# Attention sums in four column tiles with reciprocals by way of DRAM, a new order in the step, and five PSUM banks for attention where there were four

## Chip, cores, metric

One core of one Trainium2 chip. The metric is device time of one execution, in microseconds (us). A kernel's time is the median of its runs.

## The reference

Eight batches of attention over 12 heads (448 positions, head size 64), q and k normalised, then a two-layer MLP on 3584 tokens with `h - tanh(h)` between the layers; all float32.

```python
batch, n_heads, seq, head_dim = (8, 12, 448, 64)
n_tokens, d_model, d_ff = (3584, 768, 2048)
q_n, k_n = rmsnorm(q, g_q), rmsnorm(k, g_k)
attn = exp(scale * q_n @ k_n.T - max)            # per batch and head
attn = attn / (sum(attn, axis=-1) + 1e-09)
x = (attn @ v).transpose(0, 2, 1, 3).reshape(B * S, H * D)
h = x @ w_in
out = (h - tanh(h)) @ w_out
```

## The kernel before

A step is two heads of one batch: six steps make a batch, 48 steps the kernel. The MLP multiplies each layer but the second one of batch 0 as seven half-size products in place of eight (numbered 1 to 7; they run in the order 1, 4 of the tile pair before, 5, 6, 2, 7, 3). `run(gap)` emits MLP products of the batch before for so many nanoseconds. So attention is woven into the MLP from step 6 on; steps 0 to 5 (`first_slot`) have no MLP to hide in.

The kernel has eight PSUM banks in use: four hold attention, and `ma`, `mc` and two `mb` the MLP:

```python
ps_s = pool("ps_s", bufs=4, space=PSUM)
ps_m = pool("ps_m", bufs=1, space=PSUM)

def mm_bank(tag):
    return ps_m.tile([P, 512], F32, name=tag, bufs=2 if tag == "mb" else 1)
```

The sums over keys: one matmul per head with ones as weights, 64 equal rows per head, so that the reciprocal stands ready for a plain product with the values:

```python
def totals(s, dn):
    ...                                # parts: one added-up tile, or four in the first steps
    for i, p in enumerate(parts):
        for h in range(2):
            nc.tensor.matmul(
                dn[h * D : (h + 1) * D, :S], lhsT=ones[:CP, :D], rhs=p[:, h, :],
                start=(i == 0), stop=(i == len(parts) - 1),
            )
    rd = sp.tile([P, S], F32, name="rd")
    nc.vector.reciprocal(rd, dn[:, :S])
    return rd

def slot(s):                           # one woven step
    gap = gap_ns(s)
    scores(s + 1, 0); load(s + 2, "v")
    run(gap)
    norm(s + 3)                        # VectorE and GpSimd; ends with GpSimd's pow
    rd = totals(s, sc_bank())
    divide(s, values(s, sc_bank()), rd)
    run(gap)
    scores(s + 1, 1); add(s + 1)
    run(gap)
    turn(s + 2, sc_bank(), sc_bank()); norm_q(s + 3); load(s + 4, "kq")
    run(gap)
```

To evict a product is to read its sums out of its bank, which frees the bank for the next one.

```python
def factors(first):                    # operands of products 4 to 6 of the second layer
    ...
    if first:
        nc.vector.tensor_tensor(out=f1, in0=g12, in1=g11, op=ALU.subtract)     # writes tg
        nc.vector.tensor_tensor(out=f2, in0=g22, in1=f1, op=ALU.subtract)      # writes tg
        nc.gpsimd.tensor_tensor(out=g12, in0=g22, in1=g12, op=ALU.subtract)
    ...
elif p == 6:
    nc.vector.tensor_tensor(out=s2, in0=v, in1=s1, op=ALU.add)                 # evicts bank mb; then 7 adds to it
...
elif p == 3:
    nc.vector.tensor_tensor(out=s2, in0=v, in1=s2, op=ALU.add)
    def rest():                        # emitted after the next product
        shrink(up, high, s2, nc.gpsimd)                                        # writes gT
        factors(True)
    late["todo"].append(rest)
elif p == 4:
    nc.vector.tensor_tensor(out=s1, in0=v, in1=s1, op=ALU.add)                 # evicts bank mb
```

## Time and profile before

1589.97 us, median of three runs (1589.63 to 1591.56). For the comparison I cut a profiled run in three: **start**, up to the MLP's first product of batch 0; **middle**, batch 0's MLP and batch 1's first layer, up to the first `ma<-gT` product, with which batch 1's second layer begins; **weave**, from there to the last such product, with the last 33 of the 42 woven steps and a tail of plain products. In this kernel they take 120.4, 344.8 and 1105.7 us; 17.7 follow.

The page's slices of the kernel before (40 slices of 39.7 us, TensorE's busy tenths and granted clock), then from the waits of TensorE between 440 and 1480 us the only row (engine, line, what it waited for: us in all, times, longest) and one of these waits in order of time (in brackets the idle time before the instruction, and what ended it), then the reciprocals' row of the page's groups:

```profile
PE   3988768998999999999999999999999999999997
PEclk9999879999999999999999999999999999999999
```
```profile
PE mb L448 <- DVE s L530: 8.1, 6, 1.4
```
```profile
637.05 1.78 PE L448 MATMUL mb<-xT,w_f 128*128 128x224 f32 x8 [1.35 <-DVE s L530]
```
```profile
L400 DVE RECIPROCAL rd<-sc 128x448 f32<-128x448 f32 x42 | 124.0, 2953 | 34.9 <-PE sc L395 34.0
```

TensorE is full from the eighth slice or so on. From 440 to 1480 us it waits 8 us, for one thing: VectorE's line 530, the eviction of product 6, before product 7 may add to the same bank.

### The profile page before, as it was taken

Reading aid. Unit: us, or ns where it says so; the run is one execution under the profiler, and the core shown is the slowest. Engines: PE = TensorE matmul, PEld = TensorE weight load, DVE = VectorE, ACT = ScalarE, POOL = GpSimd, SP = SyncE. Lnnn points to the kernel's source line nnn. Section 1 sums busy time; section 2 is a strip of 40 time slices with the busy share of each in tenths; the row PEclk is TensorE's granted clock in tenths of the full one; section 3 lists DMA queues with packets and bytes.
Section 4 is the critical chain, followed back from the end, with each engine's and each line's share of the span. In section 5 each row is a group of like instructions: output and inputs, shape, how many; then the busy total and the mean of one; then the engine's idle time right before and its main releaser. Section 6 shows DMA issues by size and latency. Waiting matters only on the chain.

```text
span 1588.6 us, 19983 instructions
## 1 busy us (share of the span) xinstructions
PE 1494.3 (94%) x7440; PEld 1164.7 (73%) x7440; DVE 788.6 (50%) x1004; ACT 446.4 (28%) x870; POOL 624.4 (39%) x516
## 2 busy tenths in 40 slices
PE   3988768998999999999999999999999999999997
PEld 1336456446878878878877887787877887789997
DVE  6788558865454345434544445434544344522211
ACT  4554234512322223222331232321331232210210
POOL 6655446552452234422453235423444234311410
PEclk9999879999999999999999999999999999999999
DMA  7554575577545554555554564465454664455564
GB/s 193 177 181 165 195 256 166 138 196 229 164 141 161 147 151 144 152 166 148 154 170 123 158 177 131 147 184 139 137 167 133 171 166 137 135 152 162 174 196 105
DMA packets 253983, 257.80 MB, mean 162 GB/s; under 512 B 143413, under 2 KB 198709, under 8 KB 253877
## 3 DMA queue, kind: packets, MB, share of 16 engines
q1 hardware_dynamic: 253552, 256.43, 55.4%
q8 instruction: 61, 1.00, 0.3%
q14 instruction: 46, 0.37, 0.1%
q10 hardware_dynamic: 324, 0.00, 0.0%
HBM read 223.35 MB, written 33.03 MB: 161 GB/s over the span
## 4 chain that ended last, share of the span: by engine, by line
PE 74%; DVE 13%; POOL 3%; DMA 3%; issue 2%; ACT 2%; SPq 2%; ACTq 0%; DVEq 0%; POOLq 0%
PE mb L448 24%; PE ma L448 16%; PE mc L448 15%; PE sc L357 8%; PE sc L383 6%; DVE rd L400 2%; DVE w_out L79 2%; PE sc L395 2%; POOL sq L310 2%; DVE sum L376 2%; DMA w_f<-w_in 1%; PE mb L616 1%; DVE rr L311 1%; ACT p L362 1%; DVE w_out L82 1%
## 5 line engine op out<-in xcount | busy, mean ns | idle before, releaser
L362 ACT ACTIVATE p<-sc,rr 112x448 f32<-112x448 f32 x384 | 212.5, 638 | 224.0 <-PE sc L357 162.0
L448 PE MATMUL mb<-tt,w_f 128*128 128x224 f32 x768 | 166.5, 361 | 17.3 <-DMA w_f<-w_in 16.3
L357 PE MATMUL sc<-qT,kT 64*112 64x448 f32 x768 | 179.5, 574 | 2.2 <-DVE rd L400 1.5
L448 PE MATMUL ma<-xT,w_f 128*128 128x224 f32 x768 | 163.8, 365 | 11.9 <-DMA w_f<-w_in 11.9
L448 PEld LDWEIGHTS mb<-tt,w_f 128*128 128x128 f32 x768 | 142.6, 192 | 42.6 <-issue 22.8
L448 PEld LDWEIGHTS ma<-xT,w_f 128*128 128x128 f32 x768 | 149.7, 197 | 18.7 <-issue 6.2
L315 POOL TENSOR_TENSOR rr<-rr,neg_half 112x16 f32<-112x16 f32 (+1 forms) x49 | 140.7, 2871 | 51.3 <-DVE rr L314 50.3
L400 DVE RECIPROCAL rd<-sc 128x448 f32<-128x448 f32 x42 | 124.0, 2953 | 34.9 <-PE sc L395 34.0
L448 PE MATMUL ma<-gT,w_f 128*128 128x224 f32 x672 | 139.2, 356 | 0.0
L448 PEld LDWEIGHTS ma<-gT,w_f 128*128 128x128 f32 x672 | 125.3, 190 | 15.3 <-issue 15.3
L448 PE MATMUL mb<-tg,w_f 128*128 128x224 f32 x672 | 135.1, 354 | 0.0
L383 PE MATMUL sc<-p,v_nat 112*64 112x448 f32 x672 | 133.4, 539 | 0.0
L448 PEld LDWEIGHTS mb<-tg,w_f 128*128 128x128 f32 x672 | 126.2, 190 | 7.3 <-issue 7.3
L376 DVE TENSOR_TENSOR sum<-sum,p 112x896 f32<-112x896 f32 x80 | 95.8, 1198 | 58.2 <-ACT p L362 52.6
L357 PEld LDWEIGHTS sc<-qT,kT 64*112 64x112 f32 x768 | 65.9, 176 | 79.4 <-issue 62.1
L535 POOL TENSOR_TENSOR u<-u,s 128x448 f32<-128x448 f32 x32 | 36.5, 1141 | 221.0 <-DVE u L534 194.7
L311 DVE TENSOR_REDUCE rr<-sq 112x8 f32<-112x512 f32 x96 | 65.4, 681 | 113.9 <-POOL sq L310 113.9
L310 POOL TENSOR_TENSOR sq<-q_nat 112x512 f32<-112x512 f32 x48 | 50.0, 1041 | 150.5 <-DVE rr L311 103.2
L383 PEld LDWEIGHTS sc<-p,v_nat 112*64 112x64 f32 x672 | 48.3, 137 | 78.0 <-issue 78.0
L448 PE MATMUL mb<-xT,w_f 128*128 128x224 f32 x384 | 87.4, 366 | 17.2 <-DVE s L530 11.4
L504 POOL TENSOR_TENSOR gT<-s,th 128x448 f32<-128x448 f32 x64 | 75.0, 1172 | 62.1 <-ACT th L503 62.1
L448 PEld LDWEIGHTS mb<-xT,w_f 128*128 128x128 f32 x384 | 71.3, 194 | 34.6 <-issue 20.4
(108 smaller groups left out, 2146.0 us busy)
## 6 DMA issues: line engine op xcount, KB each, us to landing
w_f<-w_in SPq DMA_DIRECT2D x224, 384.0 KB, 3.6
w_f<-w_out SPq DMA_DIRECT2D x147, 512.0 KB, 4.3
w_raw<-in_moe_w_out_dram SPq DMA_DIRECT2D x32, 384.0 KB, 3.4
k_nat<-in_k_dram SPq DMA_DIRECT2D x96, 112.0 KB, 3.3
q_nat<-in_q_dram SPq DMA_DIRECT2D x48, 224.0 KB, 3.7
v_nat<-in_v_dram SPq DMA_DIRECT2D x48, 224.0 KB, 4.7
w_in<-w_out SPq DMA_DIRECT2D x28, 384.0 KB, 5.6
out_dram<-th SPq DMA_DIRECT2D x192, 56.0 KB, 2.7
```

Of the source, the lines that this page charges most:

```text
L79: nc.vector.tensor_scalar(out=bits, in0=bits, scalar1=4, scalar2=1, op0=ALU.logical_shift_left, op1=ALU.logical_shift_right)
L310: nc.gpsimd.tensor_tensor(out=sq, in0=rows, in1=rows, op=ALU.mult)
L311: nc.vector.reduce_sum(rr[:, "kq".index(name)], sq, axis=AX.X)
L315: nc.gpsimd.tensor_tensor(out=r, in0=r, in1=neg_half[:, : r.shape[1]], op=ALU.pow)
L357: nc.tensor.matmul(sc[:CP, :S], lhsT=kT[r, c * CP : (c + 1) * CP], rhs=qT[r, :], start=True, stop=True)
L362: nc.scalar.activation(p[:, h, i, :], tiles[h][:CP, :S], AF.Exp, scale=rr[:, 0, 2 * c + h : 2 * c + h + 1])
L376: nc.vector.tensor_tensor(out=t, in0=t, in1=part, op=ALU.add)
L383: nc.tensor.matmul(av[h * D : (h + 1) * D, :S], lhsT=v_nat[:, h, c, :], rhs=p[:, h, c % 2, :], start=(c == 0), stop=(c == NCH - 1),)
L400: nc.vector.reciprocal(rd, dn[:, :S])
L448: nc.tensor.matmul(bank[:, f * HS : (f + 1) * HS], lhsT=w[:, f * depth + c, :], rhs=moving[p](c), start=(first and f == 0 and c == 0), sto ...
L504: eng.tensor_tensor(out=g[:, rows, cols], in0=h, in1=th, op=ALU.subtract)
L535: nc.gpsimd.tensor_tensor(out=u3, in0=u3, in1=s5, op=ALU.add)
```

## The change

Its intent: sums in four column tiles of 32 columns (head and half of the queries) need half of TensorE's time and leave a reciprocal of half the width. The price is that each reciprocal stands on 32 rows where 64 are wanted, for half of the queries; a small store to DRAM and a load that repeats each row put that right. Sums and values each move beside half of the scores, so that there are fewer switches of tiling. And attention gets a fifth PSUM bank, taken from `mb`.

```diff
-    ps_s = pool("ps_s", bufs=4, space=PSUM)
+    ps_s = pool("ps_s", bufs=5, space=PSUM)
-        return ps_m.tile([P, 512], F32, name=tag, bufs=2 if tag == "mb" else 1)
+        return ps_m.tile([P, 512], F32, name=tag)
 ...                                                       # totals
-                nc.tensor.matmul(
-                    dn[h * D : (h + 1) * D, :S], lhsT=ones[:CP, :D], rhs=p[:, h, :], ...
+                for n in range(2):
+                    r = (2 * h + n) * BL
+                    nc.tensor.matmul(
+                        dn[r : r + BL, :HS], lhsT=ones[:CP, :BL], rhs=p[:, h, n * HS : (n + 1) * HS], ...
-        rd = sp.tile([P, S], F32, name="rd")
-        nc.vector.reciprocal(rd, dn[:, :S])
+        rs = whole[s] = sp.tile([P, HS], F32, name="rs")
+        nc.vector.reciprocal(rs, dn[:, :HS])
+    def rows_out(s):
+        row = whole[s] = scratch.tile([2, S], F32, name="row", bufs=2)
+        nc.sync.dma_start(out=row..., in_=rs.rearrange("(g i) q -> g i q", i=BL)[:, 0, :])
+    def rows_in(s):
+        rd = whole[s] = sp.tile([P, S], F32, name="rd")
+        nc.sync.dma_start(
+            out=rd,
+            in_=bass.AP(tensor=row.tensor, offset=row.offset, ap=[[S, 2], [0, D], [1, S]]),
+        )
 ...                                                       # first_slot
+        totals(s, mm_bank("mc"))                           # now first of all
         scores(s + 1, 0)
-        turn(s + 2, mm_bank("mb"), mm_bank("mb"))
+        turn(s + 2, mm_bank("mb"), sc_bank())
         load(s + 4, "kq"); norm(s + 3); weight(ahead - 2)
-        rd = totals(s, mm_bank("mc"))
         load(s + 2, "v")
+        rows_out(s)
         weight(ahead - 1)
+        rows_in(s)
         scores(s + 1, 1); add(s + 1)
 ...                                                       # slot
+        totals(s, sc_bank())
         scores(s + 1, 0); load(s + 2, "v")
-        run(gap)
+        run(gap / 2)
+        rows_out(s)
         norm(s + 3)
-        rd = totals(s, sc_bank())
-        divide(s, values(s, sc_bank()), rd)
+        run(gap / 2)
+        rows_in(s)
+        turn(s + 2, sc_bank(), sc_bank()); load(s + 4, "kq")
         run(gap)
+        divide(s, values(s, sc_bank()))
         scores(s + 1, 1); add(s + 1)
         run(gap)
-        turn(s + 2, sc_bank(), sc_bank()); load(s + 4, "kq")
         norm_q(s + 3)
         run(gap)
```

More of the change, by code (lines that the diff above doesn't have):

```diff
@@ L298, in ring_load @@
                 nc.sync.dma_start(out=t, in_=w_out_dram[:, BLOCKS[p], j].rearrange("p f d -> p (f d)"))
-    normed, turned, probs, sums, xT, tt = {}, {}, {}, {}, {}, {}
+    normed, turned, probs, sums, whole, xT, tt = {}, {}, {}, {}, {}, {}, {}
     def norm(s):
@@ L394, in totals, with divide @@
             for h in range(2):
-                nc.tensor.matmul(
-                    dn[h * D : (h + 1) * D, :S], lhsT=ones[:CP, :D], rhs=p[:, h, :],
-                    start=(i == 0), stop=(i == len(parts) - 1),
-                )
-        rd = sp.tile([P, S], F32, name="rd")
-        nc.vector.reciprocal(rd, dn[:, :S])
-        return rd
-    def divide(s, av, rd):
+                for n in range(2):
+                    r = (2 * h + n) * BL
+                    nc.tensor.matmul(
+                        dn[r : r + BL, :HS], lhsT=ones[:CP, :BL], rhs=p[:, h, n * HS : (n + 1) * HS],
+                        start=(i == 0), stop=(i == len(parts) - 1),
+                    )
+        rs = whole[s] = sp.tile([P, HS], F32, name="rs")
+        nc.vector.reciprocal(rs, dn[:, :HS])
+    def rows_out(s):
+        rs = whole[s]
+        row = whole[s] = scratch.tile([2, S], F32, name="row", bufs=2)
+        nc.sync.dma_start(
+            out=row.rearrange("h (n q) -> (h n) q", n=2), in_=rs.rearrange("(g i) q -> g i q", i=BL)[:, 0, :]
+        )
+    def rows_in(s):
+        row = whole[s]
+        rd = whole[s] = sp.tile([P, S], F32, name="rd")
+        nc.sync.dma_start(
+            out=rd,
+            in_=bass.AP(tensor=row.tensor, offset=row.offset, ap=[[S, 2], [0, D], [1, S]]),
+        )
+    def divide(s, av):
         b, hp = steps[s]
+        rd = whole.pop(s)
         x = xT[b, hp] = xp.tile([P, S], F32, name="xT")
@@ L663, in first_slot @@
     def first_slot(s):
+        if has(s):
+            totals(s, mm_bank("mc"))
         if has(s + 1):
@@ L673, in first_slot @@
         weight(ahead - 2)
-        if has(s):
-            rd = totals(s, mm_bank("mc"))
         if has(s + 2):
             load(s + 2, "v")
+        if has(s):
+            rows_out(s)
         weight(ahead - 1)
+        if has(s):
+            rows_in(s)
         if has(s + 1):
@@ L682, in first_slot @@
         if has(s):
-            divide(s, values(s, mm_bank("ma" if s < NP - 1 else "mb")), rd)
+            divide(s, values(s, mm_bank("ma" if s < NP - 1 else "mb")))
         if has(s + 3):
@@ L693, in slot @@
             load(s + 2, "v")
-        run(gap)
+        run(gap / 2)
+        rows_out(s)
         if has(s + 3):
             norm(s + 3)
-        rd = totals(s, sc_bank())
-        divide(s, values(s, sc_bank()), rd)
+        run(gap / 2)
+        rows_in(s)
+        if has(s + 2):
+            turn(s + 2, sc_bank(), sc_bank())
+        if has(s + 4):
+            load(s + 4, "kq")
         run(gap)
+        divide(s, values(s, sc_bank()))
         if has(s + 1):
@@ L703, in slot @@
         run(gap)
-        if has(s + 2):
-            turn(s + 2, sc_bank(), sc_bank())
         if has(s + 3):
             norm_q(s + 3)
-        if has(s + 4):
-            load(s + 4, "kq")
         run(gap)
```

## The prediction

> **What bounds the kernel now.** I read the page first, then busy time in stretches, the chain of waits, TensorE's weight loads in order of time, and VectorE and the DMA issues of the first 120 us.
>
> ```profile
> PE 1494.3 (94%) x7440; PEld 1164.7 (73%) x7440; DVE 788.6 (50%) x1004; ACT 446.4 (28%) x870; POOL 624.4 (39%) x516
> ...
> PE 74%; DVE 13%; POOL 3%; DMA 3%; issue 2%; ACT 2%; SPq 2%; ACTq 0%; DVEq 0%; POOLq 0%
> ```
>
> TensorE carries 74% of the chain, VectorE 13%. This average hides three stages. To about 120 us six attention steps run alone, with weight rounding; to about 400 us batch 0's MLP waits on rounding and DMA; from 400 to 1440 us 36 attention steps are woven into the MLP, and TensorE is busy 98.6 to 100% of every 100 us. Then 150 us of products alone. A batch of six woven steps repeats every 181.05 us (project's first product starts at 465.24, 646.60, 827.63). The weight loads show what an insertion of attention costs in that weave:
>
> ```profile
> 702.94 1.32 PEld L448 LDWEIGHTS ma<-gT,w_f 128*128 128x128 f32 x7
> 704.54 0.27 PEld L357 LDWEIGHTS sc<-qT,kT 64*112 64x112 f32 x4 [0.28 <-issue]
> ...
> 706.24 2.94 PEld L448 LDWEIGHTS mb<-tg,w_f 128*128 128x128 f32 x16 [0.67 <-issue]
> 709.18 2.27 PEld L448 LDWEIGHTS mc<-tg,w_f 128*128 128x128 f32 x12
> 711.73 0.20 PEld L395 LDWEIGHTS sc<-sum,ones 112*64 112x64 f32 x4 [0.28 <-issue]
> ...
> 715.64 0.68 PEld L448 LDWEIGHTS mc<-tg,w_f 128*128 128x128 f32 x4 [0.70 <-issue]
> ```
>
> From the end of one product's loads to the start of the next: half the scores take 706.24 - 704.26 = 1.98 us, sums with values 715.64 - 711.45 = 4.19; the same subtraction gives 0.86 for the turn. In the early stage VectorE is the chain, one step every 11.1 us:
>
> ```profile
> 71.10 0.17 DVE rr L314
> 71.27 2.86 DVE rd L400
> 74.13 0.22 DVE w_out L78
> 74.36 0.02 issue
> 74.38 0.37 DVE w_out L79
> 74.75 0.02 issue
> 74.78 0.71 DVE w_out L82
> 75.48 0.51 issue
> 75.99 0.98 DVE xT L406
> ```
>
> The reciprocal, one weight, then the division, all in one queue.
>
> **What the Trainium skill says.** (1) "TensorE: Matmul & The Clock Gate", Part 3, lets narrow matmuls in different column groups run at once; it measured 2.38x for three column tiles. The trace agrees for two: sixteen 64-column value instructions take 3.01 us, eight pairs of 0.376 us, what the 448 columns of one instruction take. Four tiles no run shows. (2) "TensorEngine Tiling (Array Packing)", Key Properties: changing the tiling mode drains the array. The trace agrees: loads stand 0.28 us at an entry, and an insertion costs 0.45 to 0.48 us over its pairs (1.98 against 4 x 0.376 = 1.50; 4.19 against 10 x 0.376 = 3.76). (3) "DMA: Bandwidth & Descriptors", section on why a DMA increments its semaphore by 16: a DMA spreads over k engines, k the largest number up to 16 that divides the slowest dimension of both sides. The changed broadcast reads a source of 2 x 64 (step 0) x 448, so k = 2. No transfer of before has that form. (4) The same page, Rules for kernel authors: a DMA that reads what another wrote must wait for its completion, so the two trips are in series.
>
> **The change part by part.**
>
> *Sums in four column tiles of 224.* With one added-up tile two pairs of 0.376 become two fours of 0.19: 0.37 us less per step, if four overlap as two do. With four parts (steps 0 to 7) 3.0 becomes 1.5 us, mostly where TensorE is not the bound.
>
> *Regrouping.* The order of the changed kernel's instructions shows sums+scores, turn, values+scores where there were four insertions: one insertion (0.46) saved, two switches inside gained. Scores after sums at 70.46 us stand about 0.17 us beyond the pairs, so 2 x 0.18. New cost: 0.375 + 1.50 + 0.46 + 0.18 = 2.52; 0.86; 3.01 + 1.50 + 0.46 + 0.18 = 5.15; together 8.53 against 1.98 + 1.98 + 4.19 + 0.86 = 9.01. That is 0.48 per step, times 36: **17 us**. Also, a batch has one stall of 1.36 us, TensorE waiting for an eviction behind reciprocal and additions (8.1 us, 6 times in this stage). A reciprocal 1.5 us shorter, placed elsewhere, should remove most; I take 6.
>
> *One mb bank instead of two.* Product 6 now waits for the eviction of the product 4 before it. Product 5 between gives 12 instructions x 0.19 = 2.28 us; additions end about 2.7 us after the scores, so a few short stalls: +3. In batch 0's projection tile ends fall on insertions or have ScalarE free: under +1.
>
> *Reciprocal on 224 columns.* 2.95 to about 1.48 us, 48 times; 70 us of VectorE time, of which only the early two stages have some on the path.
>
> *By way of DRAM.* A 56 KB store lands in 2.7 us, so the four rows about 2.4. A 224 KB load over all engines lands in 3.7:
>
> ```profile
> q_nat<-in_q_dram SPq DMA_DIRECT2D x48, 224.0 KB, 3.7
> ...
> out_dram<-th SPq DMA_DIRECT2D x192, 56.0 KB, 2.7
> ```
>
> On two engines each moves 64 x 1792 B = 114.7 KB. When the queues were full (60 to 71 us) they moved 362 GB/s, 22.6 per engine, so 5.1 us in place of 0.6: 8.2 us to landing. The detour is about **10.5 us** from reciprocal to rd (estimate). In the weave rows_in precedes the division by turn, a gap of products (127.7 us of products per batch / 24 = 5.3 us) and values, some 9 us, and the ring of weights runs four products ahead, so most is hidden; for ring loads queued behind it I add 3. Woven stage: -17 - 6 + 3 + 3 = **-17**.
>
> In the first six steps nothing hides it. VectorE does reciprocal, norm and one weight (2.7 + 2.2 us), then must have rd. A step becomes reciprocal 1.48 + detour 10.5 + division 1.0 + norm_q and weight about 3 = 16, against 11.1 (two lines of tt and the combinations add the same to both). That is some +4.7 for five steps; step 0's sums no longer wait for the turn, about 4.7 us earlier, so it gains back to +2.5: together **+24**. Were k = 16, the detour is 6.4 and this stage ends about even. At 3 in 4 for k = 2: **+18**.
>
> Batch 0's MLP: about four reciprocals are on the chain there, -6; SyncE, which issues every load in order, now waits there for reciprocals and for the rows' landing, and weight loads queue behind rd on two engines: +4. Net **-2**. Sum: -17 + 18 - 2 = -1, so about **1589 us**.
>
> **Rivals.** *The detour is as quick as any load* (k = 16, or weights fill the time): the start costs 0 to 5 and the gain of the weave remains, 1570 to 1577. For it: the author orders a weight between the two DMAs on purpose. Against: the form of the access pattern. *The detour chokes the queue in the weave too*: rd late at the division, VectorE in order behind it, evictions late, TensorE stalled. 1 us per step is +36, 1610 to 1625. For it: 18 us of DMA per step become some 23 on two engines, and SyncE's waits block ring loads. Against: 9 us of room, and transfers now keep four products ahead with no such wait from 400 to 1440 us. *Four column tiles do not overlap*: sums cost 0.75 as before, the regrouping alone leaves -0.1 per step; about 1602.
>
> **Range and chances.** The weave is worth -25 to +5, the start 0 to +35, the middle -10 to +8; mostly independent, they give 1568 to 1610. Faster by over 2% needs below 1558: no term is large enough unless the start gains too, 0.03. Slower by over 2%, above 1621.8, needs a late rd in the weave as well: 0.05. Within 2%: 0.92.
>
> **What would show it.** Right: sums at about 0.4 us per step in the weave; batch period near 178 us; rd landing 7 to 9 us after issue with bytes on two engines; early reciprocals 15 to 17 us apart with VectorE idle before the division for want of the DMA; the MLP's first product near 140 us, not 120.4. Wrong: rd landing near 4 us and early steps still 11 us apart (then about 1573); division waits in the weave (then over 1610); sums still near 0.8 us; new waits of mb products for the eviction of product 4 above 1 us.

## The result, and the profile after

1630.74 us (median of four timed runs, 1622.24 to 1631.78) against 1590.45 before on the same chip: 1.0247 times, 95% interval 1.0213 to 1.028. Slower, and outside the predicted range. (Such a ratio is the mean time of one kernel's fast runs over that of the other's of the same rounds, so not quite the ratio of the medians.)

The page after: busy time of the engines and the chain that ended last by engine, then the slices (of 40.5 us):

```profile
PE 1473.4 (91%) x7728; PEld 1160.1 (72%) x7728; DVE 707.0 (44%) x1004; ACT 448.6 (28%) x870; POOL 667.8 (41%) x516
...
PE   3766657998899999999999999999999999999998
PEclk9887778999999999999999999999999999999999
...
PE 69%; DVE 10%; DMA 9%; POOL 6%; issue 3%; SPq 3%; ACT 1%; DVEq 0%; POOLq 0%; ACTq 0%
```

TensorE did 21 us less and the kernel took 31 us more (this profiled run is the quick one of 1622). On the chain DMA went from 3% to 9% and GpSimd (POOL) from 3% to 6%. The slices show the loss in the first seven, with a lower clock. By stages, us of the profiled runs:

| kernel | start | middle | weave | span | clock | median |
|---|---|---|---|---|---|---|
| before | 120.4 | 344.8 | 1105.7 | 1588.6 | 0.979 | 1590 |
| after | 143.5 | 356.3 | 1103.6 | 1620.0 | 0.962 | 1631 |

So start +23, middle +11.5, weave -2. In the start, the chain of the changed kernel (start, us, what) answers to VectorE's chain in the prediction:

```profile
42.59 1.55 DVE rs L402
...
44.17 1.66 DMA row<-rs
...
45.85 7.06 DMA rd<-row
...
53.00 0.06 DVE xT L424
```

The reciprocal is 1.4 us shorter, and 8.7 us of DMA follow it. VectorE stands still before its division; from its waits over the whole run:

```profile
DVE xT L424 <- DMA rd<-row: 45.9, 9, 8.8
```

In the weave nothing waits for this load, and TensorE's waits for product 6's eviction are gone. Instead, TensorE between 440 and 1480 us waits for a new thing, nearly three times as long as for the old one:

```profile
PE mb L466 <- DVE s L564: 22.4, 11, 2.9
```

L564 is the old L546, the eviction of product 4. TensorE in order of time shows such a wait, and answers to the weight loads in the prediction:

```profile
654.30 2.45 PE L466 MATMUL mb<-tt,w_f 128*128 128x224 f32 x12
656.59 2.43 PE L466 MATMUL mc<-tt,w_f 128*128 128x224 f32 x12
661.95 1.02 PE L466 MATMUL mb<-tt,w_f 128*128 128x224 f32 x4 [2.93 <-DVE s L564]
662.90 3.23 PE L383 MATMUL sc<-p,v_nat 112*64 112x448 f32 x16
```

Product 4 into `mb`, product 5 into `mc`, then product 6 wants `mb`: there is only one, and it isn't evicted. The chain of waits at that place says why:

```profile
654.94 2.91 POOL rr L315
657.85 2.19 POOL gT L522 x2
...
660.07 0.64 DVE tg L535
...
661.27 0.63 DVE s L564
...
661.95 1.02 PE mb L466 x4
```

GpSimd runs the norm's pow (L315) for 2.9 us; behind it in its queue stand the subtractions that write `gT`; VectorE's subtraction to `tg` waits for them; and the eviction, whose product has been done for 4 us and more, stands behind that one in VectorE's queue. Such a wait of 2.9 us comes once in a batch, and another of 0.95 us.

My theories before the experiments: (a) the missing `mb` bank ate the weave's gain; (b) the load of `rd`, on two engines, is the loss of the start; (c) the middle loses by both. The rivals: the sums gained nothing; the load disturbs the weave; the new order, not the DMA, slows the start.

### The profile page after: what moved, and what is told of

The parts are those of the page before. It is cut to its first block, busy times and chain, and to the rows that moved or that the text cites. A ratio compares the mean times of both kernels' runs of the same rounds, so it can differ in the third digit from the quotient of the medians.

```text
span 1620.0 us, 20794 instructions
## 1 busy us (share of the span) xinstructions
PE 1473.4 (91%) x7728; PEld 1160.1 (72%) x7728; DVE 707.0 (44%) x1004; ACT 448.6 (28%) x870; POOL 667.8 (41%) x516
## 4 chain that ended last, share of the span: by engine, by line
PE 69%; DVE 10%; DMA 9%; POOL 6%; issue 3%; SPq 3%; ACT 1%; DVEq 0%; POOLq 0%; ACTq 0%
PE mb L466 23%; PE ma L466 15%; PE mc L466 13%; PE sc L357 8%; PE sc L383 7%; DMA rd<-row 3%; DMA w_f<-w_in 2%; POOL gT L522 2%; DVE w_out L79 2%; POOL sq L310 1%; PE sc L397 1%; DMA row<-rs 1%; DMA w_in<-w_out 1%; DVE rr L311 1%; POOL rr L315 1%
## 5 line engine op out<-in xcount | busy, mean ns | idle before, releaser
L357 PE MATMUL sc<-qT,kT 64*112 64x448 f32 x768 | 182.8, 598 | 0.6 <-ACT qT L341 0.6
L315 POOL TENSOR_TENSOR rr<-rr,neg_half 112x16 f32<-112x16 f32 (+1 forms) x49 | 140.6, 2870 | 51.3 <-DVE rr L314 47.9
L383 PE MATMUL sc<-p,v_nat 112*64 112x448 f32 x672 | 138.9, 556 | 0.0
L438 POOL TENSOR_TENSOR tt<-xT,tt 128x224 f32<-128x224 f32 x21 | 26.5, 1260 | 196.3 <-DVE xT L424 196.3
L424 DVE TENSOR_TENSOR xT<-sc,rd 128x448 f32<-128x448 f32 x42 | 40.6, 967 | 147.8 <-PE sc L383 129.4
L402 DVE RECIPROCAL rs<-sc 128x224 f32<-128x224 f32 x42 | 65.2, 1553 | 68.9 <-PE sc L397 59.1
```

What stands on the lines that cost most here:

```text
L315: nc.gpsimd.tensor_tensor(out=r, in0=r, in1=neg_half[:, : r.shape[1]], op=ALU.pow)
L357: nc.tensor.matmul(sc[:CP, :S], lhsT=kT[r, c * CP : (c + 1) * CP], rhs=qT[r, :], start=True, stop=True)
L383: nc.tensor.matmul(av[h * D : (h + 1) * D, :S], lhsT=v_nat[:, h, c, :], rhs=p[:, h, c % 2, :], start=(c == 0), stop=(c == NCH - 1),)
L402: nc.vector.reciprocal(rs, dn[:, :HS])
L424: nc.vector.tensor_tensor(out=x.rearrange("r (p c) -> r c p", c=NCH), in0=av[:, :S].rearrange("r (c p) -> r c p", c=NCH), in1=rd.rearrange ...
```

## The experiments

Twelve kernels ran, all correct, three rounds each unless said otherwise. First one part undone or repaired at a time.

**1. The eviction ahead of the subtractions.** VectorE gets the two subtractions to `tg` after the eviction of product 4, not before it:

```diff
                     def rest():
                         shrink(up, high, s2, nc.gpsimd)
-                        factors(True)
 ...                                                       # product 4
                     nc.vector.tensor_tensor(out=s1, in0=v, in1=s1, op=ALU.add)
+                    factors(True)
```

> The changed kernel, with one VectorE order turned round: product 4's eviction now stands ahead of the two subtractions for tg that wait for GpSimd; nothing else. Theory (the single mb bank makes TensorE wait for that eviction): the 22.4 us that TensorE waits for product 4's eviction between 440 and 1480 us fall below 4 us, the batch period from 180.95 to about 177.3 us, and the time by 18 to 24 us, to about 1608. Rival (the weave's gain went to the DMA detour or to insertions that cost more than I counted): the period stays within 0.7 us of 180.95 and the time within 5 us of 1630.

1592.53 us (1592.31 to 1594.81), 1.0014 of before. The waits for the eviction are gone from the weave. TensorE at the same place in order of time:

```profile
645.89 2.43 PE L466 MATMUL mc<-tt,w_f 128*128 128x224 f32 x12
648.16 0.92 PE L466 MATMUL mb<-tt,w_f 128*128 128x224 f32 x4
649.01 3.23 PE L383 MATMUL sc<-p,v_nat 112*64 112x448 f32 x16
```

Weave 1082.8 us: 20.8 less than the changed kernel and 22.9 less than before. One line moved by two places is worth 38 us in the median, far more than I expected; besides the weave, the middle got 10 us shorter. (The profiled runs differ by 29.5 us only, as the changed kernel's is the quickest of its runs: experiment 12.)

**2. Four banks for attention and two `mb`, as before, with all else changed.**

```diff
-    ps_s = pool("ps_s", bufs=5, space=PSUM)
+    ps_s = pool("ps_s", bufs=4, space=PSUM)
-        return ps_m.tile([P, 512], F32, name=tag)
+        return ps_m.tile([P, 512], F32, name=tag, bufs=2 if tag == "mb" else 1)
```

> The changed kernel with the banks as before: two for mb, four for attention. Theory: the waits for product 4's eviction vanish (-22 us), but sums and four score tiles now share four banks, so the last score tile waits for the reciprocal of the sums, up to 0.8 us in each of 36 steps (+10 to +29): 1615 to 1640. Rival (the banks have no part in the lost gain): no change of the waits, 1625 to 1635.

1647.89 us (1646.13 to 1648.47), 1.0355 of before, slower than the change and above the 1640 that I expected at most. The waits for the eviction are gone, but sums or values and half of the scores together want more than four banks; from the waits of the weight loads, a row that the changed kernel has not:

```profile
PEld sc L357 <- ACT p L362: 30.4, 42, 0.8
```

Half the scores then take 2.73 us or a little more behind the sums and some 2.14 behind the values, where experiment 1 has 1.76; that is 1.35 us a step, or 43 in the 32 steps, and the weave is 41.5 us longer than there. One step of this run in order of time:

```profile
624.26 0.59 PE L397 MATMUL sc<-sum,ones 112*32 112x224 f32 x8
624.78 2.73 PE L357 MATMUL sc<-qT,kT 64*112 64x448 f32 x8
```

So the fifth bank is needed by the new order, and the bank isn't to be given back: the eviction is to be mended.

**3. The load of `rd` as one DMA per head**, with the 64 repeats as its slowest dimension:

```diff
-        nc.sync.dma_start(
-            out=rd,
-            in_=bass.AP(tensor=row.tensor, offset=row.offset, ap=[[S, 2], [0, D], [1, S]]),
-        )
+        for h in range(2):
+            nc.sync.dma_start(
+                out=rd[h * D : (h + 1) * D],
+                in_=bass.AP(tensor=row.tensor, offset=row.offset + h * S, ap=[[0, D], [1, S]]),
+            )
```

> The changed kernel with the broadcast load of rd cut into one DMA per head of 64 partitions, so that the slowest dimension on both sides is 64 and the load spreads over all engines; same bytes, same order. Theory (two engines make it slow): rd lands in 3.5 to 4.5 us where it took 7.1 to 8.3; early reciprocals some 3 us closer; the MLP's first product at 124 to 130 us, not 143.5; the time 16 to 24 us shorter, about 1610. Rival (reading one row of DRAM 64 times is slow whatever the engines, or the two trips' fixed cost is the most of it): rd stays above 6 us, first product after 138 us, time within 6 us of 1630.

1602.20 us (1596.62 to 1606.49), 1.0058 of before. Start 143.5 to 129.5, middle 356.3 to 341.4. VectorE's waits for it over the whole run, to be read beside the 45.9 above:

```profile
DVE xT L425 <- DMA rd<-row: 7.6, 4, 4.5
```

No run tells more engines from two DMAs in place of one; but that few engines carry the load of the change shows in its own trace: from 50 to 53 us, while VectorE waits for `rd`, the DMA share is 0.11 to 0.13 of the 16 engines (two of them are 0.125), at 38 to 47 GB/s. The weave, though, got 12.8 us longer (1116.4), with no more waits; this profiled run is the slowest of its four. Experiment 12 comes back to that.

**4. The old sums and reciprocal in the first six steps**, in the new order and with no way by DRAM there:

```diff
-            totals(s, mm_bank("mc"))
+            totals_whole(s, mm_bank("mc"))                # the old totals
 ...
-        if has(s):
-            rows_out(s)
         weight(ahead - 1)
-        if has(s):
-            rows_in(s)
```

> The changed kernel whose first six steps make sums in two column tiles of 448 and take the whole reciprocal, with no DMA; order of insertions, banks and all later steps as changed. Theory (the detour alone lengthens the start): the MLP's first product at 117 to 123 us as before (120.4), not 143.5; the time 20 to 28 us shorter, about 1606. Rival (the regrouping or the single mb bank of turn lengthens the start): first product after 135 us.

1610.88 us (1609.78 to 1620.54), 1.0145 of before. The start is 127.9 us, against 117 to 123 expected: without the DMA 15.6 of the 23 us are gone, and 7.5 stay. The chain of this run names a suspect:

```profile
42.18 2.95 DVE rd L415
...
47.87 2.91 POOL rr L315
...
50.80 1.50 DVE n L321
```

The reciprocal now stands ahead of the norm in VectorE's queue. In the kernel before, norm came first and GpSimd's pow ran beside the reciprocal (pow from 60.27 us, reciprocal from 60.03); here it begins when the reciprocal and the norm's sums are done, and VectorE's next multiplication waits for it.

**5. The first six steps wholly as before** (their order too, only the turn's second bank from attention's five). The edit is that of experiment 4 with `totals_whole` back behind `norm` and the first weight.

> The changed kernel, but its first six steps are the kernel before's whole: two-tile sums, no way by DRAM, and the sums after the turn and after VectorE's norm, as before (only the turn's second bank is one of the scores' banks). The run with the old sums in the new order had its first product of the batches' work at 127.9 us, against 120.4 before and 143.5 changed. Theory (the order is the other 7.5 us: the reciprocal ahead of the norm exposes GpSimd's 2.9-us pow): first product at 120 to 122, time about 1610.9 - 7 = 1604. Rival (the bank taken from the multi-purpose pair, or GpSimd being slower beside it, holds the start): first product stays at 126 to 128, time about 1611.

1602.65 us (1600.68 to 1608.79), 1.0088 of before; start 119.4. So the order of the first steps cost 8.5 us (127.9 - 119.4), and the theory stands against the rival of the bank.

**6. The kernel before with one `mb` bank and five for attention**, and nothing else of the change:

```diff
-    ps_s = pool("ps_s", bufs=4, space=PSUM)
+    ps_s = pool("ps_s", bufs=5, space=PSUM)
-        return ps_m.tile([P, 512], F32, name=tag, bufs=2 if tag == "mb" else 1)
+        return ps_m.tile([P, 512], F32, name=tag)
-            turn(s + 2, mm_bank("mb"), mm_bank("mb"))
+            turn(s + 2, mm_bank("mb"), sc_bank())
```

> The kernel before with only the banks of the change: five for attention, one mb bank instead of two, the turn's second output in one of the attention banks; order, sums and reciprocals as before. My prediction priced the missing bank at +3 us. Theory (one bank makes TensorE wait for VectorE's eviction of the fourth product in each batch, whatever the order around it): waits of the MLP products for the s eviction go from about 8 us to over 15 us between 400 and 1440, period 182 to 184, time 1603 to 1615. Rival (the bank costs only together with the new order, which puts GpSimd's pow and gT ahead of the subtractions): 1586 to 1595.

1611.43 us (1609.76 to 1613.39), 1.0127 of before; weave 1120.7, +15.0. Its waits between 440 and 1480 us; the 8.1 of before, for product 6's eviction, are gone, and product 4's (L546) has come in (my expectation took the two for one):

```profile
PE mb L448 <- DVE s L546: 21.4, 16, 2.5
```

The bank alone, in the old order with the old sums, costs 21 us: about the size of the error of my term for it. What the eviction stands behind differs with the order: the longest stall here, 2.5 us at 641 us, follows a reciprocal and a division in VectorE's queue and not the `tg` subtractions.

**7. The kernel before with the early eviction** (edit of experiment 1):

> The kernel before with the early eviction alone. Its two banks leave only some 8 us of waits for that eviction after 440 us and 5 before. Theory (the eviction's place repairs the missing bank, and has little to give where there are two): 1578 to 1590. Rival (the early eviction is worth its 38 us by itself, and the change contributes nothing): below 1572.

1586.02 us (1585.32 to 1587.79), 0.9971 of before; weave 1102.3, -3.4. With two banks there is little to repair; the 8 us of waits are not those for product 4, as my expectation has it, but for product 6's eviction (L530), and 6.0 of them stay. The 38 us of experiment 1 mend what the change broke; they were not there to be had before.

**8. Early eviction and old first steps** (edits 1 and 5):

> As the run before, and with VectorE's eviction of the fourth MLP product placed ahead of its tg subtractions (which took 38 us from the changed kernel by itself: 1592.5). If start and weave are separate costs: 1592.5 - 23 = 1569, first product 120 to 122, batch period 176.8, faster than before by 1.3 per cent. Rival (VectorE is loaded by the early evictions and the start's gain is eaten in the middle part, as the middle of the kernel waits for DMA): above 1578.

1574.18 us (1573.17 to 1575.22), 0.9896 of before. Start 121.5, middle 351.7, weave 1082.9. Start and weave add as they should; the total is 5 above the expected sum, as the middle gained 7 and not 10, and the start came out 2 later.

**9. The same without the four-tile sums and without DRAM anywhere**: order and early eviction alone, the old `totals` in all steps.

> The new order and the early eviction with the sums over two tiles and the whole reciprocal on VectorE everywhere: no four-tile sums and nothing by way of DRAM. It says what the name-giving part of the change is worth in the batches. By my prediction the four-tile sums give 0.375 us for each of 36 steps: period 176.8 + 2.25 = 179.0, time about 1574.2 + 13.5 = 1588, less what the middle gains without the waits for the reciprocals (SyncE and VectorE), up to 8: 1580 to 1588. Rival (the sums' gain is not real, the early eviction and the order do all): period 176.5 to 177.3, time 1566 to 1575.

1581.98 us (1578.87 to 1585.79), 0.9951 of before. Weave 1096.2, so the four-tile sums are worth 13.3 us there against experiment 8. One step in each, TensorE in order of time, this kernel and then experiment 8 (the `sums` and the scores after them):

```profile
671.75 0.97 PE L410 MATMUL sc<-sum,ones 112*64 112x448 f32 x4
672.65 1.76 PE L357 MATMUL sc<-qT,kT 64*112 64x448 f32 x8
```
```profile
677.25 0.59 PE L397 MATMUL sc<-sum,ones 112*32 112x224 f32 x8
677.76 1.76 PE L357 MATMUL sc<-qT,kT 64*112 64x448 f32 x8
```

From start to start 0.90 us become 0.51: -0.39 in each of the 32 steps whose sums lie in this stage, 12.5 us; the waits for product 6's eviction (0.9 us here, none there) are the rest. The middle goes the other way: 344.0 here, 351.7 with the load on two engines.

**10. Early eviction and the load of `rd` per head** (edits 1 and 3), the changed kernel else:

> The changed kernel with both repairs that keep the way by DRAM: one DMA per head for the load of the reciprocals (16 engines instead of 2) and the early eviction. Alone they gave 1602.2 and 1592.5. If they act at separate places (load: start -14 and middle -15; eviction: weave -24 and middle -10): the sum is 1630.7 - 28.5 - 38.2 = 1564, but the load's run lost 13 us in its batches to a lower TensorE clock after the eviction's stall, which is gone here, and the middle's gains overlap by about 10, so 1555 to 1568. Theory of the clock: values of 16 products take 3.2 us again (5.4 in the run with the load alone) and the period is 176 to 177. Rival (the clock fell for the denser DMA or the load on the chip, not for the stall): values stay at 4.5 to 5.4 us, the period is over 179, time over 1577.

1570.63 us (1568.55 to 1571.72), 0.9876 of before. Start 129.5, middle 337.7, weave 1082.8: the extra 12.8 us of experiment 3's weave are gone with the stalls, so the denser DMA was not their cause. The median is 3 us above what I expected.

**11. All three repairs** (edits 1, 3 and 5):

> All three repairs: the first six steps as in the kernel before, the early eviction, and the load of the reciprocals on 16 engines for the steps after. If the start (121.5 with the old first steps), the middle (337.7 from there to the batches' regular part, as in the run with load and eviction) and the regular part (1083 to the end) add up: 1566.7 - 8 = 1559 profiled, about 1562 in the median. Rival (the weights' arrival sets the middle, and a start 8 us earlier only waits for it: the waits of MLP products for w_f rise from 53 us to about 60): 1568 to 1572.

1562.12 us (1560.24 to 1565.15), 0.9828 of before, interval 0.9811 to 0.9845. The sum was 1562. The best version found: 1.7% quicker than before, 4.2% quicker than the change as it was made (1562.12 over 1630.74).

**12. The changed kernel again**, one round:

> The changed kernel as it is, for the profile: the one that came with the result fell on the fastest of its five runs, 1622, where four had 1630 to 1633. If the difference is the TensorE clock after the stalls for the eviction, and not more stalls: a run of 1630 or more shows the same waits for the eviction, 19 to 25 us, and a lower clock (0.955 to 0.960), with values or scores of 4 to 5 us in place of 3.2. If it is more waiting: waits over 30 us at the same clock of 0.962.

1628.84 us (two timed runs, 1625.22 and 1632.45); the profile fell on the quicker one again, with clock 0.959. Its waits for the eviction in the weave come at the same places and lengths as in the first profile. TensorE at the stall shown for the first profile:

```profile
658.02 1.86 PE L466 MATMUL mb<-tt,w_f 128*128 128x224 f32 x4 [2.92 <-DVE s L564]
659.81 5.58 PE L383 MATMUL sc<-p,v_nat 112*64 112x448 f32 x16
```

The same values (x16) took 3.23 us there and 5.58 us here. The granted clock was 0.54 between 660 and 665 us, where the first profile had 1.00. After the 2.9-us stalls from 630 us on, three of five are followed by such slow work here, none in the first profile; the weave is 6.4 us longer for it (1110.0). In experiment 3 all five are (values of 4.0 to 5.5 us): that is where its 12.8 us went, and experiment 10 agrees, as it has neither stalls nor slow values. Experiments 4 and 5 have the same five stalls from 590 us on and no slow values after them.

The stages of all profiled runs, us:

| kernel | start | middle | weave | span | clock | median |
|---|---|---|---|---|---|---|
| 1 early eviction | 144.4 | 345.9 | 1082.8 | 1590.5 | 0.969 | 1592.5 |
| 2 two mb, four sc | 143.7 | 360.6 | 1124.3 | 1645.6 | 0.967 | 1647.9 |
| 3 load per head | 129.5 | 341.4 | 1116.4 | 1604.4 | 0.966 | 1602.2 |
| 4 old sums at the start | 127.9 | 359.0 | 1103.6 | 1607.7 | 0.972 | 1610.9 |
| 5 old start | 119.4 | 358.3 | 1103.7 | 1598.7 | 0.974 | 1602.7 |
| 6 before, one mb | 122.3 | 350.6 | 1120.7 | 1611.6 | 0.974 | 1611.4 |
| 7 before, early eviction | 122.1 | 344.0 | 1102.3 | 1585.9 | 0.979 | 1586.0 |
| 8 edits 1, 5 | 121.5 | 351.7 | 1082.9 | 1572.7 | 0.972 | 1574.2 |
| 9 edits 1, 5, old sums | 121.2 | 344.0 | 1096.2 | 1579.0 | 0.979 | 1582.0 |
| 10 edits 1, 3 | 129.5 | 337.7 | 1082.8 | 1566.7 | 0.970 | 1570.6 |
| 11 edits 1, 3, 5 | 119.5 | 338.8 | 1083.2 | 1558.6 | 0.980 | 1562.1 |
| 12 the change again | 144.1 | 351.8 | 1110.0 | 1623.0 | 0.959 | 1628.8 |

## Why the prediction was wrong

**The weave: -17 predicted, -2 in one profile and +4 in the other.** The terms, each from the pair of kernels that comes nearest to isolating it:

| term | predicted | measured | from |
|---|---|---|---|
| sums in four tiles | -13.5 | -13.3 | experiments 9 to 8 |
| regrouping, -3.5, and the stall that was there (L530), -6 | -9.5 | -9.5 | before to 9 (which also trades a bank and moves an eviction) |
| one mb bank | +3 | +20.8 | 8 to 5 (+15.0 in the old order: before to 6) |
| loads of weights behind `rd` | +3 | 0 | 8 to 11 (1082.9, 1083.2) |
| clock after the stalls | none | 0 to +6.4 | after, 12 |

The predicted terms are for 36 steps, of which the first three or four lie in my middle. Of the -9.5, 5.9 are waits for product 6's eviction (6.8 us in the weave before, 0.9 in experiment 9, none in 8); the regrouping alone no pair isolates.

The step that failed is "Product 6 now waits for the eviction of the product 4 before it ... so a few short stalls: +3". It found the right wait and then sized it from the wrong queue. I asked when VectorE's additions end after the scores. I didn't ask what stands ahead of the eviction in VectorE's queue and what *that* waits for: a subtraction that needs GpSimd, which is busy with a pow of 2.9 us. With a second `mb` bank that chain has slack: in the profile of before no product waits for product 4's eviction at all. With one bank there are ten stalls in the weave, 2.9 or 0.95 us each, 19.4 us in all. The gain of the weave, by contrast, came as reckoned: without the late eviction (experiment 8) it is -22.8 where the terms without the bank and the load give -23, and the old wait for product 6's eviction, of which a reciprocal shorter and elsewhere "should remove most", is gone. My list of signs did name this one, "new waits of mb products for the eviction of product 4 above 1 us", but neither rival nor range gave it weight.

**The start: +24 on two engines, weighted to +18; measured +23.** The size is right, its working only in part. Store and load took 1.66 + 7.06 us where I had 2.4 + 8.2. The two engines are 14.0 of the 23 (experiment 3 against the change). Another 8.5 were the order of the first steps (4 to 5), which I had counted as a small gain for step 0: I did not see that GpSimd's pow loses the reciprocal that it ran beside. For the same reason "Were k = 16 ... ends about even" is wrong: with that load the start is 129.5, 9 above before. The weighting by 3 in 4 cost 6 us of the error and was no mistake by itself. Its sum is not clean: five steps of 4.7 and 2.5 for step 0 are 26, not 24; that it came out so near to 23 is in part luck, as the order was left out. (Two more slips, without effect: 4.19 against 3.76 is 0.43 and not 0.45, and the detour with all engines would be 10.5 - 8.2 + 3.7 = 6.0, not 6.4.)

**The middle: -2 predicted for batch 0's MLP; +11.5 and +7 in the two profiles, batch 1's first layer included.** A gain of the predicted size is there once the rest is mended: 337.7 to 338.8 in experiments 10 and 11, 6 to 7 below before, as I had for the shorter reciprocals (-6); no run takes them apart from the rest. Against it stand the late eviction (6.6 from 5 to 8, 10.4 in experiment 1) and the load on two engines (12.9 from 8 to 11), for which I had under +1 and +4.

**The rivals.** "The detour chokes the queue in the weave too" gave nearly the right time, 1610 to 1625, for a wrong reason: the load costs nothing there. "Four column tiles do not overlap" is refuted by 0.39 us a step. "The detour is as quick as any load" described a kernel that the change is not, and could be made into, with the eviction mended too (experiment 10).

**What stays open.** The stages of the two profiles add up to 1620 and 1623; runs of 1630 to 1633, with clocks of 0.956 to 0.960, were not caught in a profile. The clock accounts for the direction, and I have not shown where those last 5 to 8 us (against the 1625.22 of the second profile) lie. Why a stall of the same length lowers the clock in one run and not in another isn't settled either.

## What to carry to other kernels

When a change takes away a second buffer, look for the instruction that frees the remaining one, and walk back through everything ahead of it *in its engine's queue*, and through what those wait for on other engines; the profile of before need not show that chain at all (here no product waited for it). To know which of several like instructions a wait names, go by the line number and read that line. When work moves within an in-order queue, list what ran beside it on other engines in the old order, for that loses its cover. And a load that repeats few rows should have the repeats, not the rows, as its slowest dimension (here 14.0 us in six steps).

## What the Trainium skill lacked or had wrong

- "DMA: Bandwidth & Descriptors", the section on why a DMA increments its semaphore by 16: its rule for the number of engines explains the load on two engines, and the runs agree (a DMA share of 0.11 to 0.13 while VectorE waits for it; 7.06 us for 224 KB in two rows; 45.9 us of VectorE's waits, against 7.6 us with the repeats slowest). What it lacks is what a small number of engines costs in time: two DMAs of 64 repeats in place of one of 2 x 64 save 14.0 us in six steps here.
- "TensorEngine Tiling (Array Packing)", Key Properties, says that a change of tiling mode drains the array, without a cost. An insertion with one kind of tiling cost 0.43 to 0.48 us over its products here.
- "TensorE: Matmul & The Clock Gate", Part 1, "What's actually happening", has the clock fall after at least one idle window of about 3.4 us. Stalls of 2.92 us were enough here: from 630 us on, slow products follow three of five of them in one run (clock 0.54 in the 5 us after one), five of five in experiment 3, and none of five in another run of the changed kernel and in experiments 4 and 5. In experiment 6 slow products follow a stall of 2.17 us too (clock 0.60 in the 4.2 us after it, at 1008 us). The stalls of 0.95 us never showed it from 580 us on.
- No page that I read has this: a stall of TensorE that comes from the order of two instructions in VectorE's queue can be worth more than an engine's whole saving. In the weave one moved eviction gave 20.8 us; four-tile sums gave 13.3.
